# Spectrum of the first convolution held on chip in data rows, and the last inverse step of group 0 placed ahead of the next step of group 1

## The chip, the cores and the metric

The kernel runs on one core of a Trainium2 chip. The metric is the device time of one execution in microseconds (us), as the median of several runs; lower is better. The engines are named as in the profile: PE (TensorE matmul), PEld (TensorE weight load), DVE (VectorE), ACT (ScalarE), POOL (GpSimd) and SP (SyncE, which here only issues DMAs). SPq is SP's queue of instructions.

## What is computed

Two kinds of layers alternate, A, B, A, B, on x of 2048 x 512 in bf16. A is a dilated sliding-window attention (32 heads of 16, eight keys per query, two rows apart). B is a long convolution along the sequence, done as an FFT:

```python
x = x + _A_ref(_layernorm(x), A_wqkv, A_wo)
x = x + _B_ref(_layernorm(x), ...)
x = x + _A_ref(_layernorm(x), A_wqkv, A_wo)
x = x + _B_ref(_layernorm(x), ...)

# _B_ref, cut: K depends on the weights alone
K  = einsum("dn,dnl,dn->dl", Cc, exp(dt * A * l), dt * Bc).real
Kf = rfft(pad(K, L)); Uf = rfft(pad(u, L))
y  = irfft(Uf * Kf)[:L] + u * Dskip
```

The weights of both B layers are the same, so the spectrum Kf is too.

## The kernel before

**Order of the work.** `k_gen` makes the convolution kernel K together with the front of the first attention. `LayerA.core` is the attention. Then comes the FFT of layer 0 (lines 1137 to 1162), the second attention (1168), and the FFT of layer 1 (1170 to 1193). "Layer 0" and "layer 1" below mean the two B layers.

**The FFT, class FftB.** The 512 channels are two groups (g = 0 and 1) of 64 x 4. Each group passes through four steps, each of which makes tiles of 128 x 1024 in PSUM (2 banks each, a pool of four tiles, all named pb) and moves them to SBUF with an eviction on ACT or DVE (`evac`, line 639, which profile rows show as L644):

- f1 (lines 646 to 657): first forward step, eight tiles of 16 matmuls, evicted to a1s. Weights are the data, in columns of 64.
- f2 (659 to 666): second forward step, eight tiles (ec = 0 to 7) of 16 matmuls with weights from w2 (w_sb in rows).
- for the convolution kernel, `k_f2` (668 to 673) evicts the f2 tile to kf_sb (three buffers of the pool wk) and stores it to kf_dram with a DMA on SP (L672). For the data, `u_f2` (675 to 695) loads the K tile back with two DMAs (L690), evicts the f2 tile to ub on ACT (L692, three buffers), and makes two products on DVE, t1 = ub x kc[0] (L693) and t2 = ub x kc[1] (L694). Rows of an f2 tile are real and imaginary parts in turn; the two loads put the real part of K into both rows for kc[0] and the imaginary part into both for kc[1].
- i1 (697 to 712): first inverse step, eight tiles of 16 matmuls: t1 with Wp (L708) and t2 with WpJ (L709), evicted to z. Each tile reads all eight e-blocks of t1 and t2, so the first waits for the last product of its group. z of group 0 lies in xnT, so its rows show xnT.
- i2 (714 to 732): last inverse step, four tiles of 12 matmuls (L722 adds x by an identity, L723 and L724 read z), evicted to x_sb. Each tile reads all of z of its group.

**Ring of K tiles.** In layer 0 kf_ring lies in the memory of k_perm (the permuted K, tag "kp", 128 x 8192) and has four slots of two halves. In layer 1 a second pool gives four more slots. A slot is loaded again once L694 has read it.

**What sets the order.** Generators are interleaved by hand: `zip_run` (594) takes one tile of each in turn, the first `lead` tiles of the first generator beforehand. Outside `manual_schedule` the framework orders each engine's instructions from this order and its own estimates, so an engine's order need not be the program's; each engine, and SP's queue, then runs in order. `fb.pat` gives the engine of each next eviction in turn.

```python
1143 zip_run(fb.f1(1, kp, "ka"), fb.k_f2(0), lead=2)
1144 zip_run(fb.f1(0, u, "ua"), fb.k_f2(1), lead=2)
1146 zip_run(fb.f1(1, u, "ua"), fb.u_f2(0), lead=2)
1147 zip_run(fb.u_f2(1), fb.i1(0), lead=4)
1152 zip_run(fb.i1(1), fb.i2(0, None), lead=2)
```

**Memory of the attention.** `LayerA.keep` has a tile with the tag "slot" that first holds the q and k weights (wqk, which `front_w`, lines 163 to 165, loads) and kT, and later w2 (`load_w2`, 460 to 464, of 128 x 16384). qT has two buffers of 128 x 2048. wv (line 214) holds the v weights.

Of the kernel before, what the change touches and what calls it, by code (L numbers as in the profile page):

```python
# [11 lines left out]
ALU = mybir.AluOpType  # L12
# [3 lines left out]
BF16 = mybir.dt.bfloat16  # L16
# [3 lines left out]
P = 128  # L20
S = 2048
D = 512
# [3 lines left out]
NA = 16  # L26
NDT = 4
# [8 lines left out]
DQG = 64  # L36
EC = 16
NEC = 128 // EC
# [84 lines left out]
class LayerA:  # L123
# [88 lines left out]
            self.kT[:, ft, e0:e1, 1:P], self.kT[:, ft, e0 + 16:e1 + 16, 0:P - 1])  # L212

    def load_wv(self, pool):
        self.wv = pool.tile([P, NDT, D], BF16, name="wv")
        self.nc.sync.dma_start(self.wv[:], self.wsrc[:, :, 2 * D:3 * D])

    def load_wo(self, pool):
# [239 lines left out]
            u_apply(14, range(14, 16))  # L458

    def load_w2(self, w2_dram):  # L460
        w2 = self.keep.tile([P, P * P], BF16, name="w2_sb", tag="slot")
        self.w2 = w2[:].rearrange("p (e c) -> p e c", c=P)
        for c in range(4):
            self.nc.sync.dma_start(self.w2[:, c * 32:(c + 1) * 32, :], w2_dram[:, c * 32:(c + 1) * 32, :])

    def close_logits(self):
        self.lctx.close()
# [13 lines left out]
def build_b_consts(nc, cpool, tmp, w2_dram):  # L481
# [29 lines left out]
    def off_cols(name, rcol, v00, v10, v01, v11):  # L511
        o = tmp.tile([P, 2], F32, name=name)
        nc.vector.tensor_scalar(o[:, 0:1], rcol, float(v10 - v00), float(v00), ALU.mult, ALU.add)
        nc.vector.tensor_scalar(o[:, 1:2], rcol, float(v11 - v01), float(v01), ALU.mult, ALU.add)
        return o
# [2 lines left out]
    eo = tmp.tile([P, 1], F32, name="w2_eo")  # L518
    nc.vector.scalar_tensor_tensor(eo[:], ak, 64.0, d4k, ALU.mult, ALU.mult)
    nc.vector.tensor_tensor(off[:], off[:], eo[:].to_broadcast([P, 2]), ALU.add)  # L520
    wps = (("Wp", (4, 8, 0, 4)), ("WpJ", (8, 12, 4, 8)))
    wo = {name: off_cols("off_" + name, rim, *offs) for name, offs in wps}
    zt = tmp.tile([P, 1024], BF16, name="w2_zero")
    nc.gpsimd.memset(zt[:], 0.0)
# [69 lines left out]
def zip_run(*gens, lead=0):  # L594
    gens = [iter(g) for g in gens]
    for _ in range(lead):
        next(gens[0], None)
    alive = list(gens)
    while alive:
        for g in list(alive):  # L600
            try:
                next(g)
            except StopIteration:
                alive.remove(g)


class FftB:
# [58 lines left out]
            yield  # L666

    def k_f2(self, g):
        def consume(p2, ec):
            kf = self.wk.tile([P, DQG, EC], BF16, name="kf_sb")  # L670
            self.evac(kf[:], p2[:].rearrange("p e q -> p q e"))
            self.nc.sync.dma_start(self.kf_dram[g, ec].rearrange("p r q e -> (p r) (q e)"), kf[:].rearrange("p q e -> p (q e)"))  # L672
        yield from self.f2(g, "ka", consume)

    def u_f2(self, g):
        nc = self.nc
        if self.kf_ring is None:
            self.kf_ring = [self.ring_pool.tile([P, 4, 2, DQG, EC], BF16, name="kf_ring", tag="kp")]
            if self.ring2 is not None:
                self.kf_ring.append(self.ring2.tile([P, 4, 2, DQG, EC], BF16, name="kf_ring2"))  # L680
        t1 = self.gtile("t1", [P, DQG, P])
        t2 = self.gtile("t2", [P, DQG, P])
        self.S[g]["t"] = (t1, t2)

        def consume(p2, ec):
            ring, slot = self.kf_ring[self.nkf // 4 % len(self.kf_ring)], self.nkf % 4
            kc = ring[:, slot]
            self.nkf += 1
            for h in range(2):
                nc.sync.dma_start(ring[h::2, slot], self.kf_dram[g, ec])  # L690
            ub = self.wk.tile([P, DQG, EC], BF16, name="ub")
            nc.scalar.copy(ub[:], p2[:].rearrange("p e q -> p q e"))  # L692
            nc.vector.tensor_tensor(t1[:, :, ec * EC:(ec + 1) * EC], ub[:], kc[:, 0], ALU.mult)  # L693
            nc.vector.tensor_tensor(t2[:, :, ec * EC:(ec + 1) * EC], ub[:], kc[:, 1], ALU.mult)  # L694
        yield from self.f2(g, "ua", consume)

    def i1(self, g):
# [353 lines left out]
def kernel(  # L1051
# [16 lines left out]
    nc = tc.nc  # L1068
# [19 lines left out]
    la = LayerA(tc, nc, consts, lnst, A_wqkv, A_wo, 0, xnT, 2)  # L1088

    C = {}  # L1090
    with tc.manual_schedule(engines={ET.DVE, ET.Activation, ET.PE, ET.SP}):
        k_gen(tc, nc, consts["ident"], ins, kd, la, x_v, lnst, lambda sp: build_b_consts(nc, cpool, sp, w2_dram), C)
# [4 lines left out]
    kpp = krctx.enter_context(tc.tile_pool(name="kp", bufs=1))  # L1097
    kp = kpp.tile([P, P, NA, 4], BF16, name="k_perm", tag="kp")
# [38 lines left out]

    z0 = xnT[:].rearrange("p t c -> p (t c)").rearrange("p (m c) -> p m c", m=2 * NA)
    fb = FftB(tc, nc, C, consts["ident"], w2_dram, g2_dram, kf_dram, x_sb, 0)
    fb.z0, fb.ring_pool, fb.w2 = z0, kpp, la.w2  # L1140
    fb.open_mid()
    zip_run(fb.f1(0, kp, "ka"))
    zip_run(fb.f1(1, kp, "ka"), fb.k_f2(0), lead=2)
    zip_run(fb.f1(0, u, "ua"), fb.k_f2(1), lead=2)
    fb.pat = ("act", "act", "act", "dve")
    zip_run(fb.f1(1, u, "ua"), fb.u_f2(0), lead=2)
    zip_run(fb.u_f2(1), fb.i1(0), lead=4)
    fb.pat = ("act", "dve")
    fb.c_mid.close()
    la.close()  # L1150
    la = LayerA(tc, nc, consts, lnst, A_wqkv, A_wo, 1, xnT, 1)
    zip_run(fb.i1(1), fb.i2(0, None), lead=2)
    fb.swap_psum()
    la.front_open()
    la.front_w()

    def rows_done(t):
        la.front_block(t, x_sb[:, t * 4:(t + 1) * 4, :], "dve", ["dve"] * 4, ["act"] * 6, "dve")
# [12 lines left out]
    fb = FftB(tc, nc, C, consts["ident"], w2_dram, g2_dram, kf_dram, x_sb, 1)  # L1171
    fb.z0, fb.ring_pool, fb.w2 = z0, None, la.w2
    fb.open_mid()
    zip_run(fb.f1(0, u, "ua"))
    fb.pat = ("act", "act", "act", "dve")
    zip_run(fb.f1(1, u, "ua"), fb.u_f2(0), lead=2)
    zip_run(fb.u_f2(1), fb.i1(0), lead=4)
    fb.pat = ("act", "dve")
# [4 lines left out]
    def store(g):  # L1183
        gs = slice(g * 4 * DQG, (g + 1) * 4 * DQG)

        def rows(t):
            for a in ((t * 4, t * 4 + 2) if (g, t) == (1, 3) else (t * 4,)):
                a1 = a + (2 if (g, t) == (1, 3) else 4)
                nc.sync.dma_start(out_v[:, a:a1, gs], x_sb[:, a:a1, gs])
        return rows  # L1190

    zip_run(fb.i1(1), fb.i2(0, store(0)), lead=2)
    zip_run(fb.i2(1, store(1), ("act", "dve", "act", "both")))
    fb.c_ps.close()
    fb.c_grp.close()
# [30 lines left out]
```

## Time and profile before

| What | Value |
|---|---|
| Median of 3 runs | 516.36 us (514.65 to 519.14) |
| Profiled execution, its own time | 513.64 us |
| Its span, first to last instruction | 511.9 us |
| Mean granted TensorE clock | 0.939 |
| Busy PE, DVE, ACT | 379.2, 414.7, 336.5 us |
| FFT of layer 0, first f1 matmul to last i2(1) eviction | 228.1 to 316.1 us |
| FFT of layer 1, first f1 matmul to last i2(1) eviction | 451.1 to 508.6 us |
| First and last K store in the SP queue | 238.26 and 260.4 us |
| DMA moved from 236 to 292 us | 13.50 MB, mean 241 GB/s |

The times in every view are us from the start of the span, in one profiled execution. The busy digits of the slices are tenths of a slice of 12.8 us. In the chain, each piece is followed by the one that it released. In a timeline, the number in brackets is how long the engine stood idle before the instruction, and what it waited for. A matmul is shown from its start to its modelled end, so the distance of two starts tells the pace and the length does not.

### The profile page before, as it was taken

How to read it: one execution, taken by the hardware profiler on the slowest of the kernel's cores; microseconds unless marked ns; L12 is line 12 of the kernel's file. 1: busy time of each engine (PE TensorE's matmuls, PEld its weight loads, DVE VectorE, ACT ScalarE, POOL GpSimd, SP SyncE). 2: the span in 40 equal slices, each digit the busy share in tenths (PEclk: the TensorE clock that was granted, in tenths of full speed). 3: DMA queues.
4: the chain of work that ended last, by engine and by line, in shares of the span. 5: the costliest groups of instructions: out<-in, count | busy, mean ns of one | idle time of the engine just before them, and what ended most of it. 6: DMA issues, size and time to landing. Idle time of an engine off the chain costs nothing.

```text
span 511.9 us, 12810 instructions
## 1 busy us (share of the span) xinstructions
PE 379.2 (74%) x5528; PEld 283.9 (55%) x5528; DVE 414.7 (81%) x580; ACT 336.5 (66%) x538; POOL 35.1 (7%) x38
## 2 busy tenths in 40 slices
PE   1000428898998998888876596889998898877795
PEld 1000216665655776667765495445657676676694
DVE  7799979999899999959776647728999999659843
ACT  5999597755554688588696534574543466679832
POOL 2000120000000011210000000100000022200000
PEclk9999978999998799899998989799997899979989
DMA  8803500111128338221788502540041061206314
GB/s 223 341 1 38 85 0 3 42 24 45 19 71 261 109 97 333 72 83 71 257 264 305 181 1 70 178 164 2 2 122 25 1 272 58 79 7 193 139 44 123
DMA packets 56122, 56.40 MB, mean 110 GB/s; under 512 B 28573, under 2 KB 45570, under 8 KB 54786
## 3 DMA queue, kind: packets, MB, share of 16 engines
q1 hardware_dynamic: 55922, 55.46, 34.8%
q8 instruction: 43, 0.70, 0.6%
q10 hardware_dynamic: 144, 0.13, 0.2%
q14 instruction: 13, 0.11, 0.1%
HBM read 38.67 MB, written 13.24 MB: 101 GB/s over the span
## 4 chain that ended last, share of the span: by engine, by line
PE 41%; DVE 23%; ACT 20%; DMA 6%; issue 4%; SPq 2%; POOL 2%; DVEq 0%; POOLq 0%; ACTq 0%
DVE pav L343 6%; PE pp L202 6%; PE pq L296 5%; PE po L351 4%; PE pq L143 4%; PE pk L975 3%; PE L L254 3%; DVE prod L247 3%; PE pb L708 3%; PE pb L709 2%; ACT ub L692 2%; DMA kf_dram<-kf_sb 2%; POOL ln_rstd L101 2%; ACT xnT L195 2%; PE pq L363 2%
## 5 line engine op out<-in xcount | busy, mean ns | idle before, releaser
L351 PE MATMUL po<-ident,pav 128*128 128x128 bf16 x1024 | 68.3, 229 | 14.4 <-DVE pav L343 14.4
L351 PEld LDWEIGHTS <-pav 128*128 128x128 bf16 x1024 | 63.8, 103 | 22.8 <-DVE pav L343 19.2
L343 DVE TENSOR_TENSOR pav<-attn,v_ext 128x4096 bf16<-128x4096 bf16 x32 | 72.9, 2283 | 0.8 <-PE po L351 0.8
L247 DVE TENSOR_TENSOR prod<-qT,kT_ext 128x4096 bf16<-128x4096 bf16 x29 | 65.8, 2285 | 3.2 <-PE L L254 3.1
L101 POOL TENSOR_TENSOR ln_rstd<-ln_rstd,ln_mh 128x4 f32<-128x4 f32 (+1 forms) x18 | 29.4, 1634 | 291.2 <-DVE ln_rstd L100 245.2
L708 PE MATMUL pb<-Wp,t 128*128 128x128 bf16 x256 | 36.0, 237 | 12.1 <-DVE t L693 7.4
L202 PE MATMUL pp<-xnT,kT_ext 128*128 128x512 bf16 x128 | 34.4, 416 | 7.2 <-ACT xnT L195 6.9
L644 ACT CAST a1s<-pb 128x1024 bf16<-128x1024 f32 x34 | 34.1, 1029 | 7.7 <-PE pb L655 6.8
L354 ACT CAST oT<-po 128x512 bf16<-128x512 f32 x32 | 18.5, 579 | 30.9 <-PE po L351 30.9
L193 PE MATMUL pt<-ident,x_blk 128*128 128x128 bf16 x64 | 5.6, 241 | 41.5 <-ACT x_blk L118 41.5
L709 PE MATMUL pb<-WpJ,t 128*128 128x128 bf16 x256 | 35.2, 237 | 0.4 <-DVE t L694 0.4
L664 PE MATMUL pb<-a1s,w_sb 128*128 128x64 bf16 x768 | 29.6, 194 | 7.9 <-ACT ub L692 4.2
L363 PE MATMUL pq<-wop,oT 128*128 128x512 bf16 x128 | 34.9, 397 | 0.0
L975 PE MATMUL pk<-B_t,A_t 128*64 128x84 bf16 (+1 forms) x512 | 25.3, 210 | 12.3 <-issue 9.3
L692 ACT CAST ub<-pb 128x1024 bf16<-128x1024 f32 x32 | 32.1, 1058 | 2.9 <-DVE t L694 2.9
L664 PEld LDWEIGHTS <-w_sb 128*128 128x128 bf16 x768 | 26.6, 98 | 11.2 <-issue 8.8
L708 PEld LDWEIGHTS <-t 128*128 128x128 bf16 x256 | 27.1, 107 | 9.4 <-DVE t L693 9.3
L298 ACT CAST v_ext<-pq 128x512 bf16<-128x512 f32 x32 | 18.8, 586 | 20.4 <-PE pq L296 20.4
L254 PEld LDWEIGHTS <-prod 128*128 128x128 bf16 x928 | 27.4, 96 | 8.0 <-DVE prod L247 1.6
L975 PEld LDWEIGHTS <-A_t 128*64 128x64 bf16 (+1 forms) x512 | 23.1, 110 | 15.6 <-issue 12.4
L296 PE MATMUL pq<-wv,xnT 128*128 128x512 bf16 x128 | 30.4, 379 | 0.0
L143 PE MATMUL pq<-xnT,kT_ext 128*128 128x512 bf16 x128 | 30.4, 380 | 0.0
(204 smaller groups left out, 883.3 us busy)
## 6 DMA issues: line engine op xcount, KB each, us to landing
kf_ring<-kf_dram SPq DMA_DIRECT2D x64, 256.0 KB
w_sb<-w_dram SPq DMA_DIRECT2D x8, 1024.0 KB
w_dram<-w_zero SPq DMA_DIRECT2D x1, 4096.0 KB
kf_dram<-kf_sb SPq DMA_DIRECT2D x16, 256.0 KB
v_ext<-v_ext SPq DMA_DIRECT2D x4, 784.0 KB
x_blk<-in_A_x_dram SPq DMA_DIRECT2D x4, 512.0 KB
kT_ext<-in_A_wqkv_dram SPq DMA_DIRECT2D x4, 512.0 KB
x_sb<-in_A_x_dram SPq DMA_DIRECT2D x4, 512.0 KB
```

Source lines behind the costliest of these rows:

```text
L143: nc.tensor.matmul(pq[:], lhsT=self.wqk[:, dt, ft * P:(ft + 1) * P], rhs=self.xnT[:, dt, q * 512:(q + 1) * 512], start=(dt == 0), stop=(dt ...
L202: nc.tensor.matmul(pp[:], lhsT=self.wqk[:, dt, D + ft * P: D + (ft + 1) * P], rhs=self.xnT[:, dt, b * 512:(b + 1) * 512], start=(dt == 0), ...
L247: nc.vector.tensor_tensor(pr, self.qT[q][:, ft].unsqueeze(1).to_broadcast([P, W, 4, P]), kap, ALU.mult)
L254: self.nc.tensor.matmul(L[:, al, w, ft * 8:(ft + 1) * 8], lhsT=pr[:, w, al, :], rhs=self.c["ind8"][:], start=False, stop=True, skip_group_ ...
L296: nc.tensor.matmul(pp[:], lhsT=xnT[:, dt, a * P:(a + 1) * P], rhs=wv[:, dt, :], start=(dt == 0), stop=(dt == NDT - 1))
L343: nc.vector.tensor_tensor(pv[:], attn[:, n % 4].unsqueeze(2).to_broadcast([P, W, DH, H]), vap, ALU.mult)
L351: nc.tensor.matmul(po[:, ft, :], lhsT=pvf[:, w, ft * P:(ft + 1) * P], rhs=ident[:], start=(w == 0 and ft == 0), stop=(w == W - 1), skip_gr ...
L363: nc.tensor.matmul(pw[:], lhsT=oT[:, ftp, :], rhs=wo[:, ftp, :], start=False, stop=(ftp == NDT - 1))
L664: nc.tensor.matmul(p2[:, j, :], lhsT=self.w2[:, ec * EC + j, :], rhs=a1s[:, ec * EC + j, :], start=True, stop=True)
L708: nc.tensor.matmul(p3[:, j, :], lhsT=t1[:, dql, :], rhs=wp_r, start=True, stop=False)
L709: nc.tensor.matmul(p3[:, j, :], lhsT=t2[:, dql, :], rhs=wpj_r, start=False, stop=True)
L975: nc.tensor.matmul(o, lhsT=lhs, rhs=Bt[:, ri, c * CH + ql].rearrange("p b g -> p (b g)"), start=(not half and j % 4 == 0 and ri == 0), sto ...
```

## The change

1. In layer 0, the sixteen K tiles are evicted to places that stay: `spare()` gives nine of them (three behind w2, whose tile is made as large as its slot, two in each of the qT buffers, two in wv's buffer), four lie in the upper half of k_perm's memory, and the last three are kf_sb. They keep the rows as f2 makes them. The store to kf_dram remains, for layer 1.
2. The products use K in these rows: t1 = ub x kn and t2 = ub x ks, where ks has real and imaginary rows exchanged. In layer 0, ks is made by two DMAs from SBUF to SBUF of 64 rows of 2 KB, into four slots in the lower half of k_perm's memory. In layer 1, three DMAs load kn and ks from kf_dram (one for the even rows of both, two for the odd rows). Wp and WpJ get other offsets for this.
3. The pattern of evictions during u_f2(0) and u_f2(1) puts the third of four on DVE, and no longer the fourth.
4. i2(0) becomes the first generator of the last interleaving, with lead 1, and i1(1) the second, in both layers. In layer 0 `front_w` is called before it.

```diff
     def load_w2(self, w2_dram):
-        w2 = self.keep.tile([P, P * P], BF16, name="w2_sb", tag="slot")
-        self.w2 = w2[:].rearrange("p (e c) -> p e c", c=P)
+        w2 = self.keep.tile([P, NDT * (2 * D + (NA + 14) * P)], BF16, name="w2_sb", tag="slot")
+        self.w2 = w2[:, 0:P * P].rearrange("p (e c) -> p e c", c=P)
+        self.w2_rest = w2[:, P * P:]
...
+    def spare(self):
+
+        rest = [self.w2_rest] + [self.keep.tile([P, 2 * DQG * EC], BF16, name=f"kn_{i}", tag="qT", bufs=2)[:] for i in range(2)]
+        rest.append(self.wv_pool.tile([P, 2 * DQG * EC], BF16, name="kn_2", tag="wv")[:])
+        n = DQG * EC
+        return [r[:, i * n:(i + 1) * n].rearrange("p (q e) -> p q e", e=EC) for r in rest for i in range(r.shape[-1] // n)]
...
-    wps = (("Wp", (4, 8, 0, 4)), ("WpJ", (8, 12, 4, 8)))
+    wps = (("Wp", (4, 12, 0, 8)), ("WpJ", (8, 8, 4, 4)))
...
     def k_f2(self, g):
+        if g == 0:
+            self.nat = list(self.spare)
+        else:
+            kp2 = self.ring_pool.tile([P, 8, DQG, EC], BF16, name="kf_nat", tag="kp")
+            self.kf_ring = kp2
+            self.nat += [kp2[:, 4 + i] for i in range(4)]
+
         def consume(p2, ec):
-            kf = self.wk.tile([P, DQG, EC], BF16, name="kf_sb")
-            self.evac(kf[:], p2[:].rearrange("p e q -> p q e"))
-            self.nc.sync.dma_start(self.kf_dram[g, ec].rearrange("p r q e -> (p r) (q e)"), kf[:].rearrange("p q e -> p (q e)"))
+            n = g * NEC + ec
+            if n >= len(self.nat):
+                self.nat.append(self.wk.tile([P, DQG, EC], BF16, name="kf_sb")[:])
+            kf = self.nat[n]
+            self.evac(kf, p2[:].rearrange("p e q -> p q e"))
+            self.nc.sync.dma_start(self.kf_dram[g, ec].rearrange("p r q e -> (p r) (q e)"), kf.rearrange("p q e -> p (q e)"))
         yield from self.f2(g, "ka", consume)
+
+    def kf_pair(self, g, ec):
+
+        n, sync = self.nkf, self.nc.sync
+        self.nkf += 1
+        if self.tag == 0:
+            kn, ks = self.nat[n], self.kf_ring[:, n % 4]
+            for h in range(2):
+                sync.dma_start(ks[h::2], kn[1 - h::2])
+            return kn, ks
+        if self.kf_ring is None:
+            self.kf_ring = [pool.tile([P, 4, 2, DQG, EC], BF16, name=f"kf_ring{i}")
+                            for i, pool in enumerate((self.ring_pool, self.ring2))]
+        kc = self.kf_ring[n // 4 % 2][:, n % 4]
+        sync.dma_start(kc[0::2], self.kf_dram[g, ec])
+        for r in range(2):
+            sync.dma_start(kc[1::2, r], self.kf_dram[g, ec, :, 1 - r])
+        return kc[:, 0], kc[:, 1]
...
         def consume(p2, ec):
-            ring, slot = self.kf_ring[self.nkf // 4 % len(self.kf_ring)], self.nkf % 4
-            kc = ring[:, slot]
-            self.nkf += 1
-            for h in range(2):
-                nc.sync.dma_start(ring[h::2, slot], self.kf_dram[g, ec])
+            kn, ks = self.kf_pair(g, ec)
             ub = self.wk.tile([P, DQG, EC], BF16, name="ub")
             nc.scalar.copy(ub[:], p2[:].rearrange("p e q -> p q e"))
-            nc.vector.tensor_tensor(t1[:, :, ec * EC:(ec + 1) * EC], ub[:], kc[:, 0], ALU.mult)
-            nc.vector.tensor_tensor(t2[:, :, ec * EC:(ec + 1) * EC], ub[:], kc[:, 1], ALU.mult)
+            nc.vector.tensor_tensor(t1[:, :, ec * EC:(ec + 1) * EC], ub[:], kn, ALU.mult)
+            nc.vector.tensor_tensor(t2[:, :, ec * EC:(ec + 1) * EC], ub[:], ks, ALU.mult)
...
-    fb.z0, fb.ring_pool, fb.w2 = z0, kpp, la.w2
+    fb.z0, fb.ring_pool, fb.w2, fb.spare = z0, kpp, la.w2, la.spare()
...
-    fb.pat = ("act", "act", "act", "dve")
+    fb.pat = ("act", "act", "dve", "act")
...
-    zip_run(fb.i1(1), fb.i2(0, None), lead=2)
+    la.front_w()
+    zip_run(fb.i2(0, None), fb.i1(1), lead=1)
     fb.swap_psum()
     la.front_open()
-    la.front_w()
...
-    fb.pat = ("act", "act", "act", "dve")
+    fb.pat = ("act", "act", "dve", "act")
...
-    zip_run(fb.i1(1), fb.i2(0, store(0)), lead=2)
+    zip_run(fb.i2(0, store(0)), fb.i1(1), lead=1)
```

More of the change, by code (lines that the diff above doesn't have):

```diff
@@ L214, in load_wv @@
     def load_wv(self, pool):
-        self.wv = pool.tile([P, NDT, D], BF16, name="wv")
+        self.wv_pool = pool
+        self.wv = pool.tile([P, NDT, D], BF16, name="wv", tag="wv")
         self.nc.sync.dma_start(self.wv[:], self.wsrc[:, :, 2 * D:3 * D])
@@ L668, in k_f2 @@
     def k_f2(self, g):
-        def consume(p2, ec):
-            kf = self.wk.tile([P, DQG, EC], BF16, name="kf_sb")
-            self.evac(kf[:], p2[:].rearrange("p e q -> p q e"))
-            self.nc.sync.dma_start(self.kf_dram[g, ec].rearrange("p r q e -> (p r) (q e)"), kf[:].rearrange("p q e -> p (q e)"))
-        yield from self.f2(g, "ka", consume)
+        if g == 0:
[4 more added lines that the diff above has]
+            self.nat += [kp2[:, 4 + i] for i in range(4)]
+        def consume(p2, ec):
+            n = g * NEC + ec
[4 more added lines that the diff above has]
+            self.nc.sync.dma_start(self.kf_dram[g, ec].rearrange("p r q e -> (p r) (q e)"), kf.rearrange("p q e -> p (q e)"))
+        yield from self.f2(g, "ka", consume)
+    def kf_pair(self, g, ec):
[14 more added lines that the diff above has]
+        return kc[:, 0], kc[:, 1]
     def u_f2(self, g):
         nc = self.nc
[L677 to L680, printed above, removed]
         t1 = self.gtile("t1", [P, DQG, P])
```

## The prediction

> **What bounds the kernel now.** I read the page first (slices, chain), then the waits, then the timelines of DVE, ACT, PE and SP inside the two FFT stretches, because the diff touches nothing else. They run from 228 to 312 us (layer 0, where the spectrum of the convolution kernel is also made) and from 451 to 512 us (layer 1). No engine is full there: the chain goes from one to the next. From the page, part 2:
>
> ```profile
> PE   1000428898998998888876596889998898877795
> DVE  7799979999899999959776647728999999659843
> ACT  5999597755554688588696534574543466679832
> DMA  8803500111128338221788502540041061206314
> ```
>
> A slice is 12.8 us; the 19th to 22nd (230 to 282 us) are the only long stretch with DMA at 7 to 8 tenths. The chain of work that ended last, inside 236 to 262 us, shows what that DMA does:
>
> ```profile
> 237.10 1.14 DVE kf_sb L644
> 238.26 2.43 DMA kf_dram<-kf_sb
> 241.95 1.23 DVE kf_sb L644
> 243.19 3.94 DMA kf_dram<-kf_sb
> 247.23 1.24 DVE kf_sb L644
> 248.48 3.49 DMA kf_dram<-kf_sb
> 252.09 1.24 DVE kf_sb L644
> 253.34 2.41 DMA kf_dram<-kf_sb
> 255.88 1.24 DVE kf_sb L644
> ```
>
> kf_sb has three buffers, so an eviction of a spectrum tile waits until the store of the tile three before it has landed: 12.3 us of chain in four stores. Then the windows view of three stages, layer 0 above layer 1 (u_f2(0); u_f2(1) with i1(0); i1(1) with i2(0)). Columns: us, then busy us of PE, PEld, DVE, ACT, POOL, granted clock, DMA share, GB/s:
>
> ```profile
> 260.55:270.76 10.21, 8.19 (x224) 7.36 (x224) 9.64 (x14) 10.21 (x12) 0.00 (x0) 1.00 0.82 260
> 270.76:288.54 17.78, 12.54 (x208) 11.34 (x207) 10.13 (x16) 11.95 (x13) 0.35 (x1) 0.90 0.70 238
> 288.54:308.39 19.85, 15.49 (x176) 14.37 (x176) 10.95 (x12) 7.59 (x8) 0.00 (x0) 0.83 0.21 69
> 460.43:470.64 10.21, 7.81 (x211) 7.08 (x209) 9.39 (x15) 10.21 (x12) 0.00 (x0) 1.00 0.53 150
> 470.64:483.61 12.97, 10.74 (x208) 9.95 (x207) 10.86 (x18) 12.20 (x13) 0.00 (x0) 1.00 0.58 209
> 483.61:500.95 17.34, 14.22 (x178) 13.42 (x179) 9.79 (x12) 7.04 (x8) 0.00 (x0) 0.90 0.17 47
> ```
>
> The same work takes 10.21 us in both layers in the first stage (ACT full), but 17.78 against 12.97 and 19.85 against 17.34 in the next two. Last, the PE timeline where the third stage begins, in layer 0 and in layer 1 (in brackets the idle time before, and who ended it):
>
> ```profile
> 288.32 0.22 PE L709 MATMUL pb<-WpJ,t 128*128 128x128 bf16 x1
> 292.86 0.50 PE L708 MATMUL pb<-Wp,t 128*128 128x128 bf16 x3 [4.32 <-DVE t L693]
> 486.73 0.50 PE L708 MATMUL pb<-Wp,t 128*128 128x128 bf16 x3 [3.12 <-DVE t L693]
> ```
>
> i1(1) needs the last products of u_f2(1), so PE stands still; afterwards its matmuls start 0.107 us apart instead of 0.056, until 299.0 and until 490.15 us.
>
> **The change, part by part.** (1) Stores off the path. The sixteen K tiles of layer 0 get places of their own (nine in spare SBUF, four in the old k_perm buffer, three kf_sb buffers), so no eviction waits for a store. What is left sets the pace: a pair of f1 and f2 tiles takes PE 1.14 us (f2 starts at 236.02, 237.15, 238.29, 239.43), DVE 1.14 us (three evictions in 3.49 us), ACT 0.92 us. From the first K eviction (237.02) DVE has 15 evictions up to the last: 237.02 + 15 x 1.14 + 1.22 = 255.3 us. It now ends 259.20 + 1.23 = 260.43. Gain 5.1 us; 3 to 6, since PE and DVE are equally tight and PSUM has four tiles. DVE's and ACT's waits for stores (3.7 and 1.8 us) say the same.
>
> (2) u_f2(0): ACT-bound at 10.21 us in both layers, so nothing.
>
> (3) u_f2(1) with i1(0). In layer 0 it shares the DMA engines with 512 KB per tile read back for the ring; DVE waits on it three times (1.7 us), PE then runs thin (1.76 us of 3 at 273 to 276 us), its clock drops, and PE, ACT and PSUM tiles wait for one another. Layer 1, whose first eight tiles are prefetched, needs 12.97 us: a gain of 17.78 - 12.97 = 4.8, if the new transfer keeps up. It is two SBUF-to-SBUF copies of 128 KB per tile into four slots: half the bytes. A slot comes free when L694 has read it and is wanted four tiles later; with L693 and L694 at 0.60 us each that leaves 3 x 1.2 + 0.6 = 4.2 us (the first product reads the unswapped tile). The way round is 0.1 us of semaphore, two issues of about 0.5 us on SP (the L690 median is 0.587) and the landing. The trace has no such copy, so: the nearest row, a 256 KB store of this same tile, landed in 2.4 us on quiet engines and in 3.5 to 3.9 at a share of 0.7 to 0.9. The Trainium skill, "DMA: Bandwidth & Descriptors", section "Anatomy of one DMA", speaks against hoping for more from half the bytes: about 2.0 us are fixed and bytes add 1 us per 436 KB (a fit for the gpsimd path), here an estimate of 2.3 us. By the page the way round is 3.4 us and nothing is lost. By the row under load, 3.5 us, it is 4.6, a pitch of (4.6 - 0.6)/3 = 1.33 instead of 1.2, over some eight tiles that come back to back 1.1 us; with the 4.05 us that a ring load took here, 2.4 us. I take 1.1, as 256 KB per 1.2 us is a loaded DMA. Net 3.7, between 0 and 4.8.
>
> (4) i2(0) ahead of i1(1). It needs only z of group 0, whose last eviction ends at 289.80 in layer 0 and 484.87 in layer 1: about 1.26 us after the last i1(0) matmul. Two i2 tiles of 1.31 us then fill the wait, and PE is not late afterwards. From then on PE is the bound: eight i1 tiles of 0.89 and four i2 tiles of 1.31 make 12.4 us (ACT and DVE have six evictions each, 6 to 7 us). So 1.26 + 12.4 = 13.6 us replace 19.8 and 17.3: gains 6.2 and 3.7. Half of each is the gap (3.06 and 1.86 us), half the slow clock (6.1 and 3.4 us at half pace, 3.1 and 1.7 lost). Here the skill's page "TensorE: Matmul & The Clock Gate" (Part 1) is to be weighed: half clock after an idle window of about 3.4 us, full clock after one busy window. The rows are stricter: 3.12 us idle was enough, 2.42 us (before 232.49 us) was not, and at 275.1 to 278.4 us thin work alone did it. If thin work ahead of i2 cools PE anyway, one window costs 1.7 us in each layer and the sum is 3.4 smaller. I hold to the rows: 1.26 us idle leaves it warm. If that cover goes, i.e. if L694 ends over 2.6 us after z, PE waits again for the rest.
>
> (5) Edits at nothing. Wp and WpJ get other constants, same instructions. The pattern (third tile of four on DVE, not the fourth) moves one eviction per four: DVE waited 2.11 us in layer 1 for i1(0)'s fourth tile, the third was done 1.8 us earlier; but i1(0)'s last eviction, on ACT, starts i2(0), so 0 to 1 us, taken 0. In layer 1 each tile takes three loads instead of two, 24 instead of 16 in each half: the first 24 are issued from 319.5 us on at some 1.4 us each, done by 353, and SP's next work is at 369.80; the second half starts at 462.82, 24 x 0.57 us, done by 477, landed some 4 us later, and the last is wanted at 484.79. Shorter rows may slow them; it costs once the last lands later than that. front_w's two 512 KB loads were already issued at 287.64, as soon as w2 was free, so its earlier place adds nothing; behind them SP has only loads of the next layer. The products now read tiles in other places: same shape, 0.68 us.
>
> Sum: 5.1 + 3.7 + 6.2 + 3.7 = 18.7 us. The profiled execution took 513.64 us around a span of 511.9; it becomes 494.9. The median of the runs is 2.7 us above it, so 516.36 - 18.7 = 497.7, about **498 us**.
>
> **Rivals.** *Half of it.* The program's order is not the engines' order: u_f2(1) and i1(0) stand in a different interleaving on ACT in the two layers, so the 4.8 us may come from the order and not from DMA, and PE and DVE at 1.14 us each may not run gap-free. Then part 1 gives 3, part 3 nothing, one of the tails half: 3 + 0 + 6.2/2 + 3.7 = 9.8, 506.5 us. For it: DVE's 4.93 us wait at 283.91 is for PE, not DMA. Against: the gap of PE needs no luck to be filled.
>
> *The change doesn't do what it says.* The first three K tiles lie in the w2 tile; if their eviction were ordered against every read of w2, and i2(0) had to wait for evictions queued behind the products, both gains vanish but for 0 to 4 us: 514 us. Against: wqk and kT share a tile in the same way, and k-projections run 8 matmuls in 1.90 us there.
>
> *Slower: the swap replaces the wait.* Place: L694 behind the swapped copy, with four slots. Price: a way round of T makes a tile (T - 0.6)/3 us. The sixteen tiles now need about 1.5 us each (10.2 + 13.0 over 16); to eat 18.7 us they would have to need 2.7, which is T = 8.6 us, twice the slowest landing plus issue seen here. At T = 10, 3.13 us a tile: 26 lost, 516.4 + 7.5 = 524 us. For it: SP's queue is in order, a copy waiting for its slot holds every later one. Against: bytes halved, and nothing waits for the stores any more.
>
> **How the numbers follow.** Full gain 0.62 (its own range, from the bounds above and 2 us of scatter, 493 to 504), half 0.22, nothing 0.08, slower 0.08. About 1% (5.2 us) is what a measurement of this kernel can tell from no change. Faster takes the first two: 0.84; same 0.08; slower 0.08. The range of 8 in 10 leaves out the last case, most of the third and the lower edge: 491 to 511.
>
> **What would show it.** Right: no eviction of a K tile waits on a DMA, and the last one ends about 18 us after the first; u_f2(1) with i1(0) lasts 13 to 14.5 us in layer 0; PE's wait on L693 before the first i1(1) matmul is under 1 us, i2 matmuls stand before it at a pitch of 0.109, and i1(1) ends some 13.6 us after i1(0) in both layers. DMA moves about 4 MB less. Wrong: L694 waiting on a kf_nat copy, tile after tile; an ACT or DVE eviction in front of the last products; PE still at half pace after i1(0).

## The result, and the profile after

| | before | after |
|---|---|---|
| Median of the runs taken together (us) | 515.55 | 497.31 |
| Lowest and highest | 514.65, 519.14 | 496.45, 497.87 |
| Profiled execution, its span | 513.64, 511.9 | 497.08, 495.3 |
| Mean granted TensorE clock | 0.939 | 0.960 |
| DMA moved (MB) | 56.40 | 52.22 |

The ratio is 0.963 (95% interval 0.958 to 0.968): 18.2 us faster, at 497.31 where 498.0 was forecast. The total was right. Of its terms, two were right in size and, as far as the runs show, in cause (the stores, and u_f2(1) with i1(0) in layer 0), that of layer 0's third stage was right in size for a wrong cause, and that of layer 1's third stage came out at less than half. Most of what follows is about the third stage.

In the profile after, `evac` shows as L653, the two products as L722 and L723, i1 as L737 and L738, i2 as L751 to L753. The slices of the page, after:

```profile
PE   1000237888999877796997886979979898877885
DVE  7799979999999998985999757738999998658943
ACT  5999678856366667877899744764544475769942
DMA  8901610112016636512474505350230080206533
```

The long stretch of DMA at 7 to 8 tenths (19th to 22nd slice) is gone. The chain of work that ended last, in the K stage of after:

```profile
237.35 1.22 DVE a1s L653
238.57 3.49 DVE w_sb L653 x3
242.07 4.56 DVE kn L653 x4
246.63 0.04 issue
246.67 0.63 PE pb L673 x16
247.30 0.57 PE pb L664 x16
```

No DMA is in it: seven evictions of K tiles follow each other without a store between them, then PE sets the pace. The windows of the three stages, after, layer 0 above layer 1, with the columns of before:

```profile
256.50:267.40 10.90, 8.76 (x240) 7.74 (x235) 9.41 (x15) 10.90 (x14) 0.00 (x0) 1.00 0.48 174
267.40:280.40 13.00, 10.73 (x208) 9.94 (x208) 12.27 (x20) 11.62 (x14) 0.35 (x1) 1.00 0.52 176
280.40:294.50 14.10, 13.02 (x179) 11.87 (x176) 8.23 (x8) 7.69 (x8) 0.00 (x0) 1.00 0.18 62
445.50:456.40 10.90, 8.61 (x230) 7.64 (x225) 9.30 (x15) 10.90 (x14) 0.00 (x0) 1.00 0.57 160
456.40:468.80 12.40, 10.53 (x209) 9.87 (x209) 11.24 (x18) 12.00 (x14) 0.00 (x0) 1.00 0.65 202
468.80:484.40 15.60, 12.87 (x180) 11.66 (x178) 9.03 (x10) 7.05 (x8) 0.00 (x0) 1.00 0.26 69
```

Layer 0 falls from 17.78 to 13.0 and from 19.85 to 14.1 us, layer 1 in its third stage only from 17.34 to 15.6. The granted clock is 1.00 in all six. These windows don't start at the same point of the work as those of before (the first holds 14 ACT instructions against 12 and is 0.7 us longer), so the 4.8 us of the second is too much; the stages defined below give 3.2. The PE timeline where the third stage begins, after:

```profile
281.33 0.27 PE L751 MATMUL pb<-x_sb,ident 128*128 128x256 bf16 x1 [0.65 <-ACT xnT L653]
281.96 0.22 PE L737 MATMUL pb<-Wp,t 128*128 128x128 bf16 x1 [0.36 <-DVE xnT L653]
...
474.61 0.23 PE L737 MATMUL pb<-Wp,t 128*128 128x128 bf16 x1 [1.92 <-DVE t L722]
```

In layer 1 PE still waits 1.92 us. In layer 0 the wait of 4.32 us is gone, but not because two i2 tiles fill it: the first i1(1) matmul starts after two lone i2 matmuls. PE then runs i2 tiles from 282.24 us on, only 0.3 us before the last product of u_f2(1) ends (282.50). There was next to nothing to fill. Why shows in the timelines of DVE and ACT. DVE before:

```profile
283.91 1.22 DVE L644 CAST xnT<-pb 128x1024 bf16<-128x1024 f32 x1 [4.93 <-PE pb L709]
...
288.58 1.22 DVE L644 CAST xnT<-pb 128x1024 bf16<-128x1024 f32 x1 [1.04 <-PE pb L709]
289.72 0.68 DVE L693 TENSOR_TENSOR t<-ub,kf_ring 128x1024 bf16<-128x1024 bf16 x1
...
292.73 0.68 DVE L694 TENSOR_TENSOR t<-ub,kf_ring 128x1024 bf16<-128x1024 bf16 x1
```

and after:

```profile
280.69 1.22 DVE L653 CAST xnT<-pb 128x1024 bf16<-128x1024 f32 x1
281.82 0.68 DVE L723 TENSOR_TENSOR t<-ub,kf_nat 128x1024 bf16<-128x1024 bf16 x1
```

xnT is z of group 0, so these are evictions of i1(0). Before, six products stand behind the eviction of i1(0)'s eighth tile in DVE's queue, and four more behind that of the fourth, for which DVE stood still 4.93 us. After, DVE evicts the third and the seventh tile, and one product stands behind the seventh. So the last product ends 2.2 us after the last i1(0) matmul (282.50 against 280.33), where it was 5.1 (293.41 against 288.32). ACT's order changed too. Before, the last ub, which the last products read, stands behind two evictions of i1(0):

```profile
287.33 1.93 ACT L644 CAST xnT<-pb 128x1024 bf16<-128x1024 f32 x2
289.14 1.04 ACT L692 CAST ub<-pb 128x1024 bf16<-128x1024 f32 x1
```

After, it stands ahead of the last three:

```profile
277.51 1.93 ACT L721 CAST ub<-pb 128x1024 bf16<-128x1024 f32 x2
279.32 2.88 ACT L653 CAST xnT<-pb 128x1024 bf16<-128x1024 f32 x3
```

### The profile page after: what moved, and what is told of

Same layout as the page of the kernel before. It is cut to its first block, busy times and chain, and to the rows that moved or that the text cites. A ratio compares the mean times of both kernels' runs of the same rounds, so it can differ in the third digit from the quotient of the medians.

```text
span 495.3 us, 12785 instructions
## 1 busy us (share of the span) xinstructions
PE 367.5 (74%) x5492; PEld 277.2 (56%) x5528; DVE 414.5 (84%) x580; ACT 336.2 (68%) x538; POOL 35.1 (7%) x38
## 2 busy tenths in 40 slices
DMA packets 57403, 52.22 MB, mean 105 GB/s; under 512 B 28829, under 2 KB 45826, under 8 KB 56066
## 4 chain that ended last, share of the span: by engine, by line
PE 40%; DVE 24%; ACT 22%; issue 5%; DMA 3%; SPq 2%; POOL 2%; POOLq 0%; DVEq 0%; ACTq 0%
DVE pav L344 7%; PE pp L202 6%; PE po L352 5%; PE pq L297 5%; PE pq L143 4%; PE pk L1004 3%; DVE prod L248 3%; PE L L255 3%; ACT ub L721 3%; PE pb L664 3%; ACT xnT L195 2%; ACT ws L922 2%; PE pq L364 2%; ACT x_blk L118 2%; SPq L1074 2%
## 5 line engine op out<-in xcount | busy, mean ns | idle before, releaser
L352 PE MATMUL po<-ident,pav 128*128 128x128 bf16 x1024 | 67.3, 228 | 16.5 <-DVE pav L344 16.5
L352 PEld LDWEIGHTS <-pav 128*128 128x128 bf16 x1024 | 62.8, 102 | 25.1 <-DVE pav L344 21.7
L653 ACT CAST a1s<-pb 128x1024 bf16<-128x1024 f32 x34 | 34.4, 1029 | 6.0 <-PE pb L664 4.8
L202 PE MATMUL pp<-xnT,kT_ext 128*128 128x512 bf16 x123 | 32.2, 399 | 7.9 <-ACT xnT L195 7.2
L737 PE MATMUL pb<-Wp,t 128*128 128x128 bf16 x256 | 30.5, 219 | 5.1 <-DVE t L722 1.9
L721 ACT CAST ub<-pb 128x1024 bf16<-128x1024 f32 x32 | 31.9, 1076 | 0.4 <-DVE t L723 0.4
L1004 PEld LDWEIGHTS <-A_t 128*64 128x64 bf16 (+1 forms) x512 | 23.0, 110 | 15.8 <-issue 12.6
L364 PE MATMUL pq<-wop,oT 128*128 128x512 bf16 x112 | 30.1, 383 | 1.2 <-ACT oT L355 0.4
L738 PE MATMUL pb<-WpJ,t 128*128 128x128 bf16 x256 | 30.2, 219 | 0.0
L143 PE MATMUL pq<-xnT,kT_ext 128*128 128x512 bf16 x121 | 29.4, 379 | 0.5 <-issue 0.3
L255 PE MATMUL L<-ind,prod 128*128 128x8 bf16 x928 | 27.5, 166 | 1.4 <-DVE prod L248 1.3
```

The costliest lines, as they stand in the source:

```text
L143: nc.tensor.matmul(pq[:], lhsT=self.wqk[:, dt, ft * P:(ft + 1) * P], rhs=self.xnT[:, dt, q * 512:(q + 1) * 512], start=(dt == 0), stop=(dt ...
L202: nc.tensor.matmul(pp[:], lhsT=self.wqk[:, dt, D + ft * P: D + (ft + 1) * P], rhs=self.xnT[:, dt, b * 512:(b + 1) * 512], start=(dt == 0), ...
L255: self.nc.tensor.matmul(L[:, al, w, ft * 8:(ft + 1) * 8], lhsT=pr[:, w, al, :], rhs=self.c["ind8"][:], start=False, stop=True, skip_group_ ...
L352: nc.tensor.matmul(po[:, ft, :], lhsT=pvf[:, w, ft * P:(ft + 1) * P], rhs=ident[:], start=(w == 0 and ft == 0), stop=(w == W - 1), skip_gr ...
L364: nc.tensor.matmul(pw[:], lhsT=oT[:, ftp, :], rhs=wo[:, ftp, :], start=False, stop=(ftp == NDT - 1))
L653: (nc.scalar.copy if eng == "act" else nc.vector.tensor_copy)(dst, src)
```

## The experiments

The table tells where each kernel spends its time. The stages, from the PE, DVE and ACT timelines of one profiled execution: A, first f1 matmul to the end of the last K eviction; B, to the last i1(0) matmul; C, to the last i1(1) matmul; in layer 1, D from the first f1 matmul to the last of i1(0), and E to the last of i1(1). Medians and ratios stand against the kernel before on the same chip (514.9 to 515.7 us).

| Kernel | median us | ratio (95%) | A | B | C | D | E |
|---|---|---|---|---|---|---|---|
| before | 515.55 | 1 | 32.3 | 27.9 | 19.8 | 32.3 | 17.3 |
| after | 497.31 | 0.963 (0.958 to 0.968) | 27.1 | 24.7 | 14.0 | 32.1 | 15.6 |
| i2(0) first alone | 513.58 | 0.994 (0.991 to 0.997) | 33.5 | 29.1 | 18.9 | 32.2 | 15.8 |
| pattern alone | 513.84 | 0.998 (0.995 to 1.001) | 35.7 | 26.7 | 20.1 | 31.7 | 16.7 |
| spectrum on chip alone | 500.49 | 0.971 (0.967 to 0.975) | 26.0 | 24.8 | 13.8 | 32.8 | 17.5 |
| on chip, pattern | 498.04 | 0.967 (0.965 to 0.969) | 27.2 | 25.0 | 14.1 | 31.9 | 15.0 |
| on chip, i2(0) first | 498.01 | 0.966 (0.962 to 0.970) | 27.2 | 24.8 | 13.6 | 32.6 | 15.8 |
| twelve more K buffers alone | 511.93 | 0.994 (0.992 to 0.996) | 26.0 | 30.5 | 18.3 | 32.7 | 17.5 |
| queue order pinned alone | 506.04 | 0.980 (0.976 to 0.985) | 34.2 | 27.5 | 13.3 | 32.4 | 13.3 |
| K buffers, order pinned | 501.04 | 0.971 (0.966 to 0.976) | 26.0 | 28.4 | 13.4 | 33.3 | 13.3 |
| after, two swap slots | 503.45 | 0.976 (0.972 to 0.980) | 27.1 | 30.7 | 14.3 | 32.2 | 15.6 |
| after, no swap | 496.67 | 0.962 (0.957 to 0.967) | 27.2 | 24.2 | 13.7 | 30.8 | 15.6 |
| after, evictions ACT, ACT | 496.74 | 0.964 (0.961 to 0.966) | 27.2 | 24.7 | 14.0 | 31.9 | 13.5 |
| mixed | 495.17 | 0.960 (0.956 to 0.965) | 27.1 | 24.9 | 13.8 | 32.1 | 13.5 |

B to E scatter by about a microsecond between executions; A more (32.3 to 35.7 in the four kernels that store as before). "On chip" stands for parts 1 and 2 of the change, "pattern" for part 3, "i2(0) first" for part 4.

**i2(0) first, alone.**

```diff
-    zip_run(fb.i1(1), fb.i2(0, None), lead=2)
+    la.front_w()
+    zip_run(fb.i2(0, None), fb.i1(1), lead=1)
...
-    zip_run(fb.i1(1), fb.i2(0, store(0)), lead=2)
+    zip_run(fb.i2(0, store(0)), fb.i1(1), lead=1)
```

> The kernel before with only the last part of the change: i2(0) ahead of i1(1) in both layers, spectrum still read back from DRAM, old pattern of evictions. Theory (the gap of PE is filled, but the eviction of the second i2(0) tile stands on DVE ahead of the last products: of the last two pairs in layer 0, of the last pair in layer 1): layer 0 ends i1(1) only some 2.5 us earlier, layer 1 some 1.8 us earlier, together 4.3 us, about 511 us. Rival 1 (as predicted: the fill is worth 6.2 + 3.7 wherever the products stand): 9.9 us less, 505.7 us. Rival 2 (the order is worth something only with the spectrum on chip): no change, 515.5 us.

Some 2 us came of it (C 0.9, E 1.5), not 9.9, and half of what the theory gave. In layer 0 DVE now has the eviction of the second i2(0) tile ahead of the last two pairs of products, and PE waits 3.12 us for them after i2(0)'s first two tiles: the move fills a wait and makes another. DVE, then PE:

```profile
296.57 1.23 DVE L644 CAST x_sb<-pb 128x1024 bf16<-128x1024 f32 x1 [1.45 <-PE pb L724]
```

```profile
299.65 0.23 PE L708 MATMUL pb<-Wp,t 128*128 128x128 bf16 x1 [3.12 <-DVE t L693]
```

**On chip with the new pattern, i1(1) first again.**

> The changed kernel with i1(1) ahead of i2(0) again, lead 2, as before; everything else of the change stays. Theory (terms: stores 4.8 us, the middle stage of layer 0 about 4.4, and the third stage of layer 0 falls back from 14.0 to the 17.3 us of layer 1 before, that of layer 1 from 15.6 to 17.3): 5.0 us over the changed kernel, 502.3 us. Rival 1 (the predicted sizes, 6.2 + 3.7 for the order): 507 us. Rival 2 (the spectrum on chip gives nearly all): within 1 us of the changed kernel. In its trace the theory wants PE idle 3 us or more ahead of the first i1(1) matmul in both layers, and a pitch of 0.107 us after it.

0.7 us lost by the medians, 1.9 by the ratios, whose intervals meet. In layer 1 E is even shorter (15.0 against 15.6). C is 14.1 us without the move: whatever shortened layer 0's third stage, it was not the move.

**K buffers alone.** The K tiles get twelve places instead of three (nine spare ones and three kf_sb; the last four tiles take the first four places again), but are read back from DRAM through the ring.

> The kernel before with twelve buffers for K tiles instead of three (nine in the spare memory, three kf_sb, then the first four again); the tiles are still read back from DRAM into the ring in both halves. It tells the stores apart from the read-back. Theory (the stores held the evictions): the last K eviction comes 4 to 5 us earlier, and 4 to 5 us are kept: about 511 us. Rival (the DMA engines are the bound of the whole stretch, so that the stores only make way for the same 12.6 MB): the evictions come earlier, the products then wait for the ring instead, and less than 2 us are kept, 514 us or more.

A falls by 6.3 us and B grows by 2.6. DVE waits 5.27 us for i1(0)'s fourth tile, and PE 4.32 us before i1(1), as before. Freeing the stores is worth 3.8 us by itself.

**After, with ACT, ACT, DVE, ACT for i2(0)'s evictions in layer 1.** DVE's timeline of after, in layer 1, shows what makes PE wait there:

```profile
472.73 1.23 DVE L653 CAST x_sb<-pb 128x1024 bf16<-128x1024 f32 x1 [2.22 <-PE pb L753]
473.88 0.68 DVE L722 TENSOR_TENSOR t<-ub,kf_ring 128x1024 bf16<-128x1024 bf16 x1
```

The last pair of products waits behind an eviction that waits for PE.

```diff
-    zip_run(fb.i2(0, store(0)), fb.i1(1), lead=1)
+    zip_run(fb.i2(0, store(0), ("act", "act", "dve", "act")), fb.i1(1), lead=1)
```

> The changed kernel with one thing more: in layer 1 the second i2(0) tile is evicted by ACT (evictions of i2(0) on ACT, ACT, DVE, ACT). Theory (in layer 1 that eviction, on DVE ahead of the last pair of products, made PE wait 1.92 us): PE's wait disappears, the third stage of layer 1 takes 13.7 us instead of 15.6, 1.9 us less than the changed kernel, 495.4 us. Rival (PE is held by ACT or by PSUM tiles as well): same as the changed kernel within 0.5 us, 497.3 us.

PE's wait is gone and E is 13.5 us, where the prediction had 13.6. The edit also moves the fourth i2(0) tile to ACT and some evictions of i1(1) to DVE, since both share one alternation; but the wait of 1.92 us is nearly all of the 2.1 us by which E falls. The median moves by 0.6 us only, which these runs can't separate from after.

After these four I held that the pattern decides the gaps, since DVE's long wait was for i1(0)'s fourth tile, which the new pattern gives to ACT. Three runs complete the set of on chip, pattern and order.

**Old pattern, on chip, i2(0) first.**

```diff
-    fb.pat = ("act", "act", "dve", "act")
+    fb.pat = ("act", "act", "act", "dve")
```

> The kernel after, with the third and fourth eviction of four again ACT, ACT (the old pattern: fourth on DVE) during u_f2(0) and u_f2(1), in both layers. New theory: the pattern decides whether PE stands still. With the old one DVE has the eviction of i1(0)'s fourth tile in its order ahead of the last products, waits 2 us or more for it, the last pair of products is late by that, PE waits 3 us for it and then runs a while at half pace. As i2(0) now stands ahead of i1(1), part of the gap is filled: about 3.5 us worse than after, 500 to 501. Rival (the prediction's own pricing: the pattern is worth 0 to 1 us): 497.3 to 498.3, and no DVE wait of 2 us for an i1(0) tile.

The edit is the one shown: of four evictions the third goes back to ACT and the fourth to DVE.

**Pattern alone.**

> The kernel before, with nothing changed but the pattern (third of four on DVE, not fourth) during u_f2(0) and u_f2(1), in both layers. New theory: DVE's wait for i1(0)'s fourth tile (4.93 us in layer 0, 2.11 in layer 1) falls under 1 us, PE's waits for L693 before the first i1(1) matmul (4.32 and 3.12 us) fall to 2.4 or less, the half pace behind them goes, and the time falls by 4 to 7 us, to 509 to 512. Rival (the pattern is worth nothing by itself): 514.5 to 516.

**Spectrum on chip alone.**

> The kernel after, with the old pattern and with the old order of i1(1) and i2(0): only the spectrum on chip in data rows is left of the change. New theory: the K stage ends 5 us earlier as in after, u_f2(1) of layer 0 is free of the ring loads, but DVE waits about 2 us for i1(0)'s fourth tile in both layers and PE's waits before i1(1) stay at about 3 us with half pace behind them: 503 to 505. Rival A (data on chip closes the gap alone): 498. Rival B (it brings the stores only, as the kernel with twelve more K buffers did): 509 to 512.

The old pattern took 498.01 us, in its rival's range, and DVE waits at most 0.90 us for i1(0)'s fourth tile in it. The pattern alone changed nothing clear of noise, and the spectrum on chip alone took 500.49 us, less time than the 503 to 505 of the theory. So my theory fell, in layer 0. With the pattern alone PE's gap is still there, and in layer 1 it shrank from 3.12 to 2.23 us. PE's timeline of that kernel:

```profile
297.19 0.50 PE L708 MATMUL pb<-Wp,t 128*128 128x128 bf16 x3 [4.62 <-DVE t L693]
...
489.50 0.34 PE L708 MATMUL pb<-Wp,t 128*128 128x128 bf16 x3 [2.23 <-DVE t L693]
```

The spectrum on chip alone gives 14.4 of the 18.2 us and has C at 13.8, with neither pattern nor order. On top of it the pattern is worth 2.0 us and the order 2.5 by the ratios, each by itself (intervals over each other), and both show in layer 1: E goes from 17.5 to 15.0 or to 15.8. With both, E is 15.6: the order adds nothing there once the pattern is changed.

But what in "on chip" closes the gap, the absent loads or the place of the evictions? In the four kernels with the ring (before, the pattern alone, i2(0) first alone, K buffers alone), six to eight products stand in layer 0 behind DVE's last eviction of i1(0) (the eighth tile with the old pattern, the seventh with the new); in the five with tiles on chip so far, one.

**Queue order pinned, everything else as before.**

```diff
-    zip_run(fb.u_f2(1), fb.i1(0), lead=4)
+    with tc.manual_schedule(engines={ET.DVE, ET.Activation}):
+        zip_run(fb.u_f2(1), fb.i1(0), lead=4)
```

The same in both layers.

> The kernel before, with only this: during u_f2(1) with i1(0), in both layers, DVE and ACT keep the order in which the program names the instructions (all eight pairs of products ahead of the evictions of i1(0)'s fourth and eighth tile on DVE; no eviction of ub behind the last evictions of i1(0) on ACT). The spectrum still goes through DRAM and the ring. Newer theory: what made PE stand still before i1(1) is the place of i1(0)'s evictions in DVE's and ACT's queues; with them behind, PE's gaps of 4.32 and 3.12 us and the half pace after them go, the third stage takes about 14 us in both layers, and the time falls by some 9 us, less about 1 for later evictions of i1(0): 505 to 508. Rival: the loads of the ring make the last products late whatever the order: 512 to 516, with the gain in layer 1 alone at best.

9.0 us, with the ring and its loads in place: C and E are 13.3 us. DVE and then PE of this kernel at the start of the third stage:

```profile
290.27 0.69 DVE L693 TENSOR_TENSOR t<-ub,kf_ring 128x1024 bf16<-128x1024 bf16 x1 [1.00 <-DMA kf_ring<-kf_dram]
290.88 0.68 DVE L694 TENSOR_TENSOR t<-ub,kf_ring 128x1024 bf16<-128x1024 bf16 x1
291.48 2.35 DVE L644 CAST xnT<-pb 128x1024 bf16<-128x1024 f32 x2
```

```profile
291.77 0.22 PE L708 MATMUL pb<-Wp,t 128*128 128x128 bf16 x1 [0.52 <-ACT xnT L644]
```

DVE does wait for the ring, five times, 4.9 us in all. Yet the evictions stand behind the products, and PE's gap is 0.52 us. So the gap came from the place of i1(0)'s evictions in the queues and not from late loads. DVE and ACT were pinned together, and no run tells the two apart.

**K buffers with the order pinned.**

> The kernel with twelve more K buffers (stores off the path, the tiles still read back from DRAM), and DVE's and ACT's order during u_f2(1) with i1(0) pinned as in the other run of this batch. Newer theory: 3.8 us for the stores and 8 to 9 us for the order: 501 to 504, about what the kernel with only the spectrum on chip took (500.5), so that the read from DRAM itself costs little. Rival: the loads cost on their own, 4 us or more above that: 505 to 509.

501.04 us, like the spectrum on chip alone (500.49), but made differently: E is 4.2 us better and B 3.6 us worse. The windows of stage B, first of this kernel, then of the one with the spectrum on chip alone:

```profile
257.40:285.80 28.40, 22.40 (x463) 20.71 (x464) 21.53 (x33) 24.45 (x28) 0.35 (x1) 0.88 0.91 317
```

```profile
256.90:281.80 24.90, 20.11 (x465) 18.57 (x465) 22.33 (x34) 24.28 (x27) 0.35 (x1) 1.00 0.54 189
```

With the loads the DMA share is 0.91 and the granted clock 0.88; without, 0.54 and 1.00. The total was as my theory had it, but its reading, that the read from DRAM costs little, was not: the read costs about 3.5 us, near the rival's 4, though in stage B. The two kernels differ in the pinned order too; in layer 1, pinned as well, this costs D 0.5 us at most (33.3 against 32.8), which is within the scatter, so most of the 3.5 is left to the loads. No run has both the tiles on chip and the order pinned.

**Two slots for the swapped tiles.**

```diff
-            kn, ks = self.nat[n], self.kf_ring[:, n % 4]
+            kn, ks = self.nat[n], self.kf_ring[:, n % 2]
```

> The kernel after, with two slots instead of four for the swapped K tiles of layer 0. A slot is then wanted again two tiles later, so the tile pitch cannot be under (way round + 0.6)/2. If the way round is 3.1 us (0.1 of semaphore, two issues of 0.5, landing 2.0 as the chain of after shows): 1.85 us a tile instead of about 1.45 over sixteen tiles, less what the first two have in hand: 5 to 9 us slower than after, 502 to 506. If it is 4.6 us, as the prediction took it: 2.6 us a tile, 17 us slower, about 514. If under 2.3 us: no change.

By the ratios 6.6 us slower than after, and B grows by 6.0. The total lies in the range given for a way round of 3.1 us, but the rows show more. DVE waits four times for a swapped tile: from the end of the second product that frees a slot to the start of the one that needs it again it takes 3.3, 4.3, 4.7 and 3.6 us, at a DMA share of 0.45 in B. The second of these, where the product in the first row frees the slot at 272.93:

```profile
272.24 0.69 DVE L723 TENSOR_TENSOR t<-ub,kf_nat 128x1024 bf16<-128x1024 bf16 x1 [0.57 <-DMA kf_nat<-kn]
277.27 0.69 DVE L723 TENSOR_TENSOR t<-ub,kf_nat 128x1024 bf16<-128x1024 bf16 x1 [1.89 <-DMA kf_nat<-kf_nat]
```

The second products follow one another at 2.25 us on average (the first starts at 258.45, the sixteenth at 292.26). So products are late in this kernel (the last ends 6.3 us after i1(0), four of them behind DVE's last eviction of i1(0)), and here i2(0)'s first two tiles do stand in the wait: C stays at 14.3.

**No swap.**

> The kernel after without the copies that exchange real and imaginary rows in layer 0: both products read the same K tile, so the second product is left without its exchange. It measures what the copies cost. If they are hidden but for DVE's rare waits: 0 to 1 us faster than after, 496.3 to 497.5. If a tile is stretched by the copies as the prediction had it for some eight tiles: 1.1 us faster. If the way round sets the pace of all sixteen tiles: 3 us or more faster, under 494.5.

By the ratios 0.6 us faster (0.962 against 0.963, intervals over each other), with B 0.5 us shorter. The copies are hidden.

**Mixed:** old pattern and order in layer 0; in layer 1 the new ones and i2(0)'s evictions on ACT, ACT, DVE, ACT.

> The kernel after with the old pattern and the old order of i1(1) and i2(0) in layer 0, and in layer 1 the new ones with i2(0)'s evictions ACT, ACT, DVE, ACT. By stages: from the first f1 matmul to the last of i1(1), layer 0 took 64.6 us in the kernel with only the spectrum on chip and 65.7 in after, layer 1 45.4 us with ACT, ACT and 47.7 in after. If the stages simply add up: 1.1 + 2.3 = 3.4 us faster than after, 494. If 1.1 us in layer 0 is no more than scatter between executions: 495. If neither carries over to the median, as the run with ACT, ACT alone suggested (0.6 us): 496.5 to 497.5.

495.17 us, the lowest median of all. E is 13.5 again, 2.1 us under after; C and A to B are after's, so the 1.1 us in layer 0 was scatter. The ratio's interval (0.956 to 0.965) still overlaps that of after.

## Why the prediction was right and where it was wrong

The stages of the profiled executions fell by 5.2 (A), 3.2 (B), 5.8 (C), 0.2 (D) and 1.7 (E), together 16.1 us, of 16.6 by which these two executions differ (513.64 and 497.08). The medians differ by 18.2, because the profiled execution of before lay 1.9 us under its median.

1. *Stores off the path, 5.1 us.* Right: A fell from 32.3 to 27.1. Alone it is worth 3.8, as B then grows (27.9 to 30.5); with the order pinned its DMA share in B is 0.91, where before has 0.82 and 0.70 in the two windows of B.
2. *u_f2(0), nothing; u_f2(1) with i1(0), 3.7 us net.* Right in size: B fell from 27.9 to 24.7. That the loads cause most of it is supported by the kernel with K buffers and the order pinned (28.4 against 24.8). The loss by the copies, taken as 1.1, was about 0.5, which is within the scatter of B. Of the two ways round weighed there, 3.4 us as an estimate from the Trainium skill's "DMA: Bandwidth & Descriptors", section "Anatomy of one DMA", and 4.6 from the store's row under load, neither was clearly the better: the waits with two slots show 3.3 to 4.7 us. My formula for the stretched pitch was also wrong. Four slots ask that 4p - 0.6 be at least T, so p = (T + 0.6)/4, not (T - 0.6)/3. They agree at p = 1.2 only: a way round of 4.6 us makes a pitch of 1.30 and not 1.33, and the slower rival would have needed T = 10.2 us and not 8.6.
3. *i2(0) ahead of i1(1), 6.2 us in layer 0 and 3.7 in layer 1.* The failed step is "Two i2 tiles of 1.31 us then fill the wait". In layer 0 the 5.8 us came without the move (C 13.8 with the spectrum on chip alone), and the move alone gave 0.9, for it put an eviction that waits for PE ahead of products that PE waits for. So that this term came out right was luck. The wait itself was a matter of order in the queues: on DVE evictions of i1(0) ahead of six products, on ACT two of them ahead of the last ub. Pinning the order of both engines removed it. The trace of before showed it in the row with 4.93 us for PE, which the prediction quoted only as a point for a rival. In layer 1 the move alone gave 1.5 us of the 3.7 (E 17.3 to 15.8), and beside the new pattern nothing (15.0 to 15.6); the rest was lost to the eviction of i2(0)'s second tile on DVE, a thing listed among the signs of error and not priced. With that eviction on ACT, E is 13.5, against 13.6 in the working.
4. *The pattern, 0 to 1 us, taken 0.* Under-priced, beside the spectrum on chip: 2 us by the ratios (0.971 to 0.967, intervals over each other), in layer 1, where the eviction of i1(0)'s fourth tile leaves DVE's queue. In the profiled executions E falls by 2.5 us, of which the shorter wait (3.12 to 2.23 us) is 0.9; most of the rest is a stretch of half clock of 3.4 us, which the kernel without the new pattern has and the one with it has not. Whether a wait of this length costs such a stretch is in part chance, as the last section shows.

Against the profiled executions the sum of 18.7 was 2.1 us too high, nearly all of it in layer 1's third stage (3.7 against 1.7); that forecast and median meet to 0.7 us is in part scatter, and so luck. That DVE's order is another one with the tiles on chip is seen in the kernels; that the framework does so because it reckons the loads late is my inference, and no run tests its estimates.

## What to carry to other kernels

Where an engine waits for the last of a series, look in the producer's queue at what stands *ahead* of those last instructions: an eviction that waits for the consumer makes its own wait. Pinning the order of two engines was a few lines and gave half of what the large change gave. Before moving work into a gap, ask what the moved work puts into the other engines' queues; and when a term comes out right, test its cause apart, since here layer 0's was right for another reason.

## What the runs showed of the hardware

The clock does not follow the length of a gap alone. The same wait of 2.23 us before i1(1) in layer 1 left PE at full pace with the spectrum on chip and the new pattern (matmuls 0.055 us apart throughout), and halved it with the pattern alone, and that only 1.5 us after PE had resumed. PE's timeline of the latter:

```profile
490.83 0.22 PE L708 MATMUL pb<-Wp,t 128*128 128x128 bf16 x1
490.89 0.36 PE L709 MATMUL pb<-WpJ,t 128*128 128x128 bf16 x2
491.05 0.31 PE L708 MATMUL pb<-Wp,t 128*128 128x128 bf16 x1
491.16 0.31 PE L709 MATMUL pb<-WpJ,t 128*128 128x128 bf16 x1
491.26 0.31 PE L708 MATMUL pb<-Wp,t 128*128 128x128 bf16 x1
```

The starts go from 0.055 to 0.107 us apart. In each of the fourteen traces all changes of the granted clock, from full to half and back, lie on one grid of 3.413 us, whose place in the span differs from trace to trace. Here are the step of the grid that holds most of the wait and the step behind it, first with the pattern alone, then on chip with the new pattern (columns as in the other windows):

```profile
487.53:490.94 3.41, 1.29 (x19) 1.07 (x20) 2.51 (x5) 0.88 (x1) 0.00 (x0) 1.00 0.00 0
490.94:494.35 3.41, 3.41 (x35) 3.36 (x32) 1.23 (x1) 1.01 (x1) 0.00 (x0) 0.50 0.02 5
```

```profile
469.70:473.11 3.41, 1.67 (x25) 1.39 (x26) 2.25 (x4) 0.67 (x2) 0.00 (x0) 1.00 0.00 0
473.11:476.53 3.42, 3.42 (x56) 3.31 (x54) 1.94 (x2) 1.97 (x2) 0.00 (x0) 1.00 0.02 5
```

Of the 2.23 us, 1.97 fell into the step in the first kernel and 1.70 in the second. PE was busy for 1.29 us of the step in the one and for 1.67 in the other, and only the first step was followed by half clock. So the place of a wait on the grid helps to decide what it costs. How busy a step has to be, no run here settles. In "TensorE: Matmul & The Clock Gate", Part 1, the Trainium skill calls the window of about 3.4 us free-running, which agrees with the grid. The prediction's working with the length of a gap, "3.12 us idle was enough" and 2.42 us not, was thus too firm a reading of two rows.
